# Decode block with cached attention: three equal rooms of 64 KB rows for the load stream, one batch per partition half, last heads' work regrouped

## The chip, the cores and the metric

One core of one Trainium2 chip. The metric is the device time of one execution in microseconds, as the median of several runs; the kernel before has 698.93 us (three runs, 698.74 to 699.79). All times in the profile are counted from the start of one profiled execution.

## What is computed

One decode step of a transformer block with adaptive layer norm, for two batches (B = 2) of one token of width 512, all in float32. Attention has 32 heads of width 128 over a cache of 4096 positions; the hidden layer has 1376 units. Cut to what matters:

```python
mod = (silu(c) @ w_mod).reshape(2, 6, 1, 512)          # sa, ca, ga, sb, cb, gb
h = layernorm(x) * (1 + ca) + sa
q = (h @ wq) per head
p = softmax(q . k_cache / sqrt(128))                    # 4096 positions
x = x + ga * ((p . v_cache) over all heads @ wo)
h = layernorm(x) * (1 + cb) + sb
a = h @ w1 + b1
x = x + gb * ((a * tanh(softplus(a))) @ w2)
```

The two caches are 268 MB of the 297 MB that are read; every byte is used once. So a load stream runs through the whole kernel, and the engines work beside it.

## The kernel before

**The stream.** `stream()` (lines 28 to 64) writes down the order of all loads by hand. The pieces are K of a head and V of a head (8192 float32 a partition each, `BIG`), a quarter chunk of wq or wo (2048, `W`, for four heads) and the other weights. K of head h is followed by V of an earlier head; at heads 14 and 22 (`AHEAD`) V is left out, so that V falls two heads further behind, and three V heads are left for after the last K. `load(n)` (line 136) issues load n on the SP queue into a room of SBUF. `room(n)` (line 115) gives every third load the one room of 48 KB a partition (`one`), and the others one of two rooms of 64 KB (`two`); a `one` room holds a K or V head and, in some, wq and wo chunks, a `two` room two heads. `used(*keys)` (line 148) issues the next load as soon as all pieces of the room three loads back have been used in program order; on the chip SP then waits until the engines are done with that room. The program lists 53 input transfers.

**Batches.** Each partition holds 32 positions of batch 0 and 32 of batch 1 (`b j d`). The positions of a batch are spread over all 128 partitions.

**The loop over heads** (lines 432 to 454). For head h: `products` (L316) multiplies K by q in place on DVE, q being spread to all partitions by matmuls in `project_q` (L288, one set for each batch); `soft_max(h - 1)` (L337, L339) takes the maximum over partitions out of PSUM and makes the exponentials and their sums on ACT, once for each batch; `sums` (L319) reduces the products to scores; `row_max` (L324 to L331) takes the maxima, lays them on a diagonal (d, 128 x 256) and multiplies by ones, so that each partition sees all maxima. `weighted_v` (L365) makes p . V on PE: 16 calls for a head, each of 512 columns, four of them side by side in groups of 32 output rows; the trace shows each call as two matmuls. After four heads `value_sums` (L379) copies the sums out, `head_values` (L387) divides and turns them, and `project_o` (L395) multiplies by wo. The engines take their instructions in program order, so a matmul behind one that waits for a load waits too.

**The tail** (line 458 on). After the last K: the softmax of head 31; V of heads 29 and 30, then modulation 4 (L241, `modulation`: 16 calls), the output projection of heads 28 to 30 (`head_out_q`, L403), V of head 31, its sums, its projection; then xg = projection x mod 2 (L494), the second layer norm (`centred`, L194, with modulation 3 laid between), `h2t`, the w1 matmuls (L521), the activation (L548 to L556), the w2 matmuls (L561) and the output. `busy(n)` (L293) puts matmuls on PE whose result nobody reads. The last loads are: V28 with wo 6; V29; V30; wo 7 with m4; V31 in three parts; m3; w1 in two parts; m5; w2 in four parts (6, 3, 1 and 1 of its 11 chunks of 512). m0, m1 and m2 come first of all with wq 0 and 1.

Of the kernel before, what the change touches and what calls it, by code (L numbers as in the profile page):

```python
# [8 lines left out]
F32 = mybir.dt.float32  # L9
# [10 lines left out]
W = 2048  # L20
SIZES = {
    "k": BIG, "v": BIG, "wq": W, "wo": W, "m012": 3 * W, "m3": W, "m4": W, "m5": W,
    "w1": 4 * sum(WIDTHS), "w2": 512 * len(CHUNKS),
}
AHEAD = (14, 22)


def stream():

    behind, pieces = {}, [("k", 0)]
    for h in range(1, HEADS):
        pieces.append(("k", h))
        if h not in AHEAD:
            behind[h] = len(behind)
            pieces.append(("v", behind[h]))
    left = list(range(len(behind), HEADS))
    pieces += [("v", h) for h in left[:-1]]

    extra = {}
    for c in range(2, HEADS // HC):
        at = (pieces.index(("k", HC * c)) - 1) // 5 * 5
        extra[at] = [("wq", c), ("wo", c - 2)]
    extra[60] = [("wo", HEADS // HC - 2)]
    loads = [[([("m012", 0), ("wq", 0), ("wq", 1)], (3 * W, 2 * W))]]
    n = 0
    while n < len(pieces):
        m = 1 if n % 5 == 0 else 2
        keys = pieces[n : n + m]  # L50
        if keys[0] == ("v", left[0]) and m == 2:
            loads.append([([key], (BIG,)) for key in keys])
        else:
            keys = keys + (extra.pop(n, []) if m == 1 else [])
            loads.append([(keys, (sum(SIZES[kind] for kind, _ in keys),))])
        n += m
    assert not extra and len(loads) % 3 == 0
    last = HEADS - 1
    loads += [
        [([("wo", HEADS // HC - 1), ("m4", 0)], (2 * W,)), ([("v", last)], (BIG // 2, BIG // 4, BIG // 4))],  # L60
        [([("m3", 0), ("w1", 0)], (W, 2 * sum(WIDTHS), 2 * sum(WIDTHS)))],
        [([("m5", 0), ("w2", 0)], (W, 6 * 512, 3 * 512, 512, 512))],
    ]
    return loads, behind, left
# [3 lines left out]
def kernel(  # L68
# [5 lines left out]
    behind: dict,  # L74
    left: list,
# [19 lines left out]
    NS = BIG // (B * DH)  # L95
# [19 lines left out]
    def room(n):  # L115

        if n % 3 == 1:
            return kvp.tile([P, BIG + 2 * W], F32, tag="one", name=f"one{n}", bufs=1)
        return kvp.tile([P, 2 * BIG], F32, tag="two", name=f"two{n}", bufs=2)

    def take(t, keys):
        lo = 0
        for kind, n in keys:
            part = t[:, lo : lo + SIZES[kind]]
            lo += SIZES[kind]
            if kind in "kv":
                (k_t if kind == "k" else v_t)[n] = part.rearrange("p (b j d) -> p b j d", b=B, d=DH)
# [8 lines left out]
    def load(n):  # L136

        t = room(n)
# [126 lines left out]
    ps = modulation("0", 3, w_t["m012"])  # L265
# [16 lines left out]
    def project_q(ch):  # L282

        q_t[ch] = work.tile([P, B, HC, DH], F32, tag="q", name=f"q{ch}")
        for b in range(B):
            ps = wide_ps(f"qps{ch}_{b}")
            for k in range(G):
                nc.tensor.matmul(  # L288
                    ps, lhsT=hc[:, k, b : b + 1].to_broadcast([P, P]), rhs=wq_t[ch][:, k, :], start=(k == 0), stop=(k == G - 1)
                )  # L290
            nc.scalar.activation(q_t[ch][:, b].rearrange("p h d -> p (h d)"), ps, AF.Copy, scale=SCALE)  # L291

    def busy(n):  # L293

        for lo in range(0, n, 2):
            cols = P * min(2, n - lo)
            nc.tensor.matmul(ov[1][:, :cols], lhsT=ident, rhs=e_t[0][0].rearrange("p c m -> p (c m)")[:, :cols], start=True, stop=True)
# [5 lines left out]
    s_t, m_t, mps, l_t, lps, pick_t, o_t = {}, {}, {}, {}, {}, {}, {}  # L303

    e_t = [[const.tile([P, NB, R], F32, name=f"e{i}_{b}") for b in range(B)] for i in range(HC)]
    ot_t = [const.tile([P, HC, R], F32, name=f"ot{i}") for i in range(2)]
    for t in sum(e_t, ot_t):
        nc.gpsimd.memset(t, 0.0)
# [12 lines left out]
    def row_max(h):  # L321

        m_t[h] = work.tile([P, 4], F32, tag="m", name=f"m{h}")
        nc.vector.tensor_reduce(out=m_t[h][:, 0:2], in_=s_t[h], axis=AX.X, op=ALU.max)  # L324
        d = work.tile([P, B, P], F32, tag="d", name=f"d{h}", bufs=1)
        nc.vector.tensor_tensor(  # L326
            out=d, in0=ident[:, None, :].to_broadcast([P, B, P]),
            in1=m_t[h][:, 0:2, None].to_broadcast([P, B, P]), op=ALU.mult,
        )
# [311 lines left out]
```

## Time and profile before

| | |
|---|---|
| median of the runs | 698.93 us |
| span of the profiled execution | 697.0 us |
| around it (launch and end), median less span | 1.9 us |
| DVE busy | 595.8 us (85%) |
| PE busy | 308.2 us (44%) |
| ACT busy | 43.7 us (6%) |
| input read | 297.2 MB, 426 GB/s over the span |
| mean granted clock of TensorE | 0.713 |

The profiled execution has no time of its own beside its span; the 1.9 us are taken from the median. A row of the profile names the line, the engine, the operation, the tile written and the tiles read, and its shape; then comes the busy time, the mean of one, and the idle time of that engine ahead of it with what ended it. PEld is TensorE's weight load, which overlaps its matmuls. In a row of the timeline the first number is the start and the second the duration. "DMA share" is the mean busy share of the 16 DMA engines. "PEclk" is the clock granted to TensorE, 1 being full.

### The profile page before, as it was taken

The page shows a single profiled execution, that of the slowest core. Times are in us where ns is not written, and L with a number is a line of the kernel's source. Part 1 is how long each engine was busy: PE and PEld are TensorE (multiplying, and loading weights), DVE is VectorE, ACT ScalarE, POOL GpSimd, SP SyncE. Part 2 cuts the span into 40 slices and gives each one's busy share as a digit, 9 for nine tenths or more (in the row PEclk, how much of TensorE's full clock was granted, in tenths as well). Part 3 has the DMA queues.
Part 4 walks back from the last instruction along what each step waited for, and adds up shares of the span by engine and source line. Part 5 has one row for each costly group of instructions (what it writes and reads, how often), then busy time and mean ns, then how long its engine had stood idle before and what let it go on. Part 6 is the DMA issues. An engine that isn't in the chain of part 4 may idle for free.

```text
span 697.0 us, 4072 instructions
## 1 busy us (share of the span) xinstructions
PE 308.2 (44%) x1692; PEld 107.0 (15%) x1692; DVE 595.8 (85%) x218; ACT 43.7 (6%) x176; POOL 4.4 (1%) x22
## 2 busy tenths in 40 slices
PE   2913343523453722843034831644043832226686
PEld 1300011100110200310011200211010300002234
DVE  3399999959999769999999789999999689999501
ACT  1100000000000000010000100000000100000001
POOL 2000000000000000000000000000000000000000
PEclk9966656776556765695665865986556975666799
DMA  9999999999999999999999999999999999999996
GB/s 383 453 429 417 427 459 411 448 429 416 454 432 425 438 425 428 448 430 433 429 444 426 432 440 417 446 432 429 444 423 440 430 425 440 429 420 432 422 422 269
DMA packets 7842, 297.48 MB, mean 427 GB/s; under 512 B 1016, under 2 KB 1040, under 8 KB 1424
## 3 DMA queue, kind: packets, MB, share of 16 engines
q1 hardware_dynamic: 7648, 297.21, 98.9%
q8 instruction: 13, 0.21, 0.1%
q10 hardware_dynamic: 176, 0.01, 0.0%
q14 instruction: 5, 0.04, 0.0%
HBM read 297.22 MB, written 0.00 MB: 426 GB/s over the span
## 4 chain that ended last, share of the span: by engine, by line
DVE 72%; DMA 24%; PE 2%; issue 1%; POOL 0%; SPq 0%; ACT 0%; DVEq 0%; POOLq 0%
DVE s L319 35%; DVE two L316 25%; DMA two<-in_load 22%; DVE one L316 10%; DMA bias<-in_b1c 2%; DVE d L326 1%; PE qps L288 1%; PE modps L241 1%; DVE m L324 1%; DVE m L337 0%; DVE pick L357 0%; SPq L143 0%; DVE pick L356 0%; PE fps L263 0%; ACT q L291 0%
## 5 line engine op out<-in xcount | busy, mean ns | idle before, releaser
L316 DVE TENSOR_TENSOR two<-two,q 128x8192 f32<-128x8192 f32 x24 | 208.5, 8687 | 37.1 <-DMA two<-in_load 37.1
L319 DVE TENSOR_REDUCE s<-two 128x64 f32<-128x8192 f32 x24 | 208.2, 8675 | 0.0
L365 PE MATMUL ov<-two,e 128*32 128x512 f32 x864 | 148.0, 847 | 134.1 <-DMA two<-in_load 81.9
L331 PE MATMUL mt<-d,ones 128*128 128x256 f32 x64 | 28.6, 536 | 130.3 <-DVE d L326 130.3
L316 DVE TENSOR_TENSOR one<-one,q 128x8192 f32<-128x8192 f32 x8 | 69.5, 8685 | 7.9 <-ACT q L291 7.9
L365 PEld LDWEIGHTS ov<-two,e 128*32 128x32 f32 x864 | 33.8, 149 | 233.4 <-issue 110.3
L319 DVE TENSOR_REDUCE s<-one 128x64 f32<-128x8192 f32 x8 | 69.4, 8676 | 0.0
L339 ACT ACTIVATE e<-s,m 128x32 f32<-128x32 f32 x64 | 20.1, 314 | 483.0 <-DVE m L337 483.0
L288 PE MATMUL qps<-one,hc 128*128 128x512 f32 x96 | 45.0, 624 | 0.0
L365 PE MATMUL ov<-one,e 128*32 128x512 f32 x160 | 28.1, 867 | 32.8 <-ACT e L339 17.1
L331 PEld LDWEIGHTS mt<-d,ones 128*128 128x128 f32 x64 | 12.0, 235 | 153.5 <-DVE d L326 108.9
L348 PE MATMUL l<-l,ones 128*128 128x8 f32 (+2 forms) x18 | 5.4, 370 | 63.4 <-ACT e L339 63.4
L288 PEld LDWEIGHTS qps<-one,hc 128*128 128x128 f32 x96 | 18.9, 201 | 24.4 <-issue 24.1
L348 PEld LDWEIGHTS l<-l,ones 128*128 128x128 f32 x18 | 4.5, 312 | 68.9 <-ACT e L339 68.5
L337 DVE TENSOR_REDUCE m<-mt 128x2 f32<-128x256 f32 x32 | 13.4, 418 | 1.4 <-PE mt L331 1.4
L326 DVE TENSOR_TENSOR d<-ident,m 128x256 f32<-128x256 f32 x32 | 13.6, 425 | 1.1
L365 PEld LDWEIGHTS ov<-one,e 128*32 128x32 f32 x160 | 6.3, 154 | 52.0 <-ACT e L339 17.9
L288 PE MATMUL qps<-two,hc 128*128 128x512 f32 x32 | 14.0, 595 | 0.3 <-DVE hc L278 0.3
L387 PE MATMUL otp<-pick,o 128*128 128x8 f32 (+2 forms) x72 | 10.0, 264 | 7.6 <-DVE m L324 4.7
L291 ACT ACTIVATE q<-qps 128x512 f32<-128x512 f32 x16 | 9.4, 594 | 52.2 <-PE qps L288 52.2
L339 ACT ACTIVATION_READ_ACCUMULATOR e<-s,m 128x1 f32 x64 | 12.0, 187 | 0.0
L387 PEld LDWEIGHTS otp<-pick,o 128*128 128x128 f32 x72 | 9.2, 200 | 14.8 <-ACT o L379 9.1
(105 smaller groups left out, 95.0 us busy)
## 6 DMA issues: line engine op xcount, KB each, us to landing
one<-in_load SPq DMA_DIRECT2D x6, 6144.0 KB, 31.8
one<-in_load SPq DMA_DIRECT2D x6, 4096.0 KB, 29.7
two<-in_load SPq DMA_DIRECT2D x2, 4096.0 KB, 24.7
two<-in_load SPq DMA_DIRECT2D x3, 2048.0 KB, 14.8
one<-in_load SPq DMA_DIRECT2D x1, 5120.0 KB
two<-in_load SPq DMA_DIRECT2D x1, 3072.0 KB
two<-in_load SPq DMA_DIRECT2D x3, 1024.0 KB, 20.7
one<-in_load SPq DMA_DIRECT2D x2, 1376.0 KB
```

The costliest lines, as they stand in the source:

```text
L241: nc.tensor.matmul(ps[R * g : R * (g + 1)], lhsT=ct[:, k, :], rhs=t[:, k, :].rearrange("p (m n) -> p m n", m=n)[:, :, P * g : P * (g + 1)] ...
L288: nc.tensor.matmul(ps, lhsT=hc[:, k, b : b + 1].to_broadcast([P, P]), rhs=wq_t[ch][:, k, :], start=(k == 0), stop=(k == G - 1))
L291: nc.scalar.activation(q_t[ch][:, b].rearrange("p h d -> p (h d)"), ps, AF.Copy, scale=SCALE)
L316: nc.vector.tensor_tensor(out=k_t[h], in0=k_t[h], in1=qv, op=ALU.mult)
L319: nc.vector.tensor_reduce(out=s_t[h], in_=k_t[h], axis=AX.X, op=ALU.add)
L326: nc.vector.tensor_tensor(out=d, in0=ident[:, None, :].to_broadcast([P, B, P]), in1=m_t[h][:, 0:2, None].to_broadcast([P, B, P]), op=ALU.mult,
L331: nc.tensor.matmul(mps[h], lhsT=ones, rhs=d, start=True, stop=True)
L337: nc.vector.tensor_reduce(out=m[:, 2:4], in_=mps[h], axis=AX.X, op=ALU.max, negate=True)
L339: nc.scalar.activation(e_t[i][b][:, :, M * i + 4 * b : M * i + 4 * b + 4], s_t[h][:, b].rearrange("p (c m) -> p c m", m=4), AF.Exp, bias=m ...
L348: nc.tensor.matmul(lps[n][:, x], lhsT=ones, rhs=l_t[n][:, x], start=True, stop=True)
L365: nc.tensor.matmul(ov[bank][R * g : R * (g + 1), :], lhsT=e_t[h % HC][b][:, c, :], rhs=v_t[h][:, b, 4 * c : 4 * c + 4, :].rearrange("p m d ...
L387: nc.tensor.matmul(tps[:, x], lhsT=o_t[m], rhs=pick_t[n][:, m, x], start=(m == 0), stop=(m == 3),)
```

## The change

**One row for each load.** The rooms are three of 64 KB (`room`, line 132 after), and loads 1 to 31 are each one transfer of 64 KB a partition: one K head with as much of the following pieces as fits, where V now comes in halves of 4096 (the key is `("v", head, part)`) and a wq chunk goes with the wo chunk of two chunks earlier. Load 0 is m0 and m1 with wq 0 and 1 (32 KB), then K of head 0 (32 KB). The program lists 43 input transfers. The last ones are: V28 with wo 6; V29; V30; V31 whole; wo 7 with m2, m4 and m3; w1 whole; m5 with 5 chunks of w2; 4 chunks; 1; 1. To make room, the scratch for dynamic DMAs is set to 1024 bytes.

**One batch per partition half.** Partitions 0 to 63 hold batch 0, 64 to 127 batch 1, each with 64 positions. q is then one set of matmuls (`hcw` holds the 64 columns of each batch), the exponentials are made on 64 partitions for each batch with 64 positions each, and the maximum needs a d of 64 columns, multiplied by `same` (ones within a half). `e_t` is one tile for a head, `sum_t` two fixed tiles for the sums.

**The tail.** Modulation 0 at the start has two parts (m0, m1) rather than three; modulation 2 is now made in the tail. The sums of heads 28 to 31 are divided in one step. Order on PE: V29, V30, the sums of heads 28 to 30, V31, modulation 2, the projection of heads 28 to 30, the sums of head 31, half of modulation 4, the projection of head 31, the other half; within the layer norm m4 + 1 on DVE; modulation 3 whole after the variance, and `busy(2)` where six stood. The `busy` calls around head 31's sums are gone.

```diff
@@ -18,50 +18,48 @@
 HC = 4
 BIG = 8192
 W = 2048
+HALF = BIG // 2
 SIZES = {
-    "k": BIG, "v": BIG, "wq": W, "wo": W, "m012": 3 * W, "m3": W, "m4": W, "m5": W,
+    "k": BIG, "v": HALF, "wq": W, "wo": W, "m01": 2 * W, "m2": W, "m3": W, "m4": W, "m5": W,
     "w1": 4 * sum(WIDTHS), "w2": 512 * len(CHUNKS),
 }
 AHEAD = (14, 22)
+ROW = 2 * BIG
 
 
 def stream():
 
 
-
...
+    order, n_v = [], 0
     for h in range(1, HEADS):
-        pieces.append(("k", h))
+        order.append(("k", h))
+        if h % HC == HC - 1 and HC < h < HEADS - 1:
+            c = (h + 1) // HC
+            order.append([("wq", c), ("wo", c - 2)])
         if h not in AHEAD:
...
+            order += [("v", n_v, 0), ("v", n_v, 1)]
+            n_v += 1
+    order = [x if isinstance(x, list) else [x] for x in order]
+
+    def size(x):
+        return sum(SIZES[key[0]] for key in x)
+
+    loads = [[([("m01", 0), ("wq", 0), ("wq", 1)], (4 * W,)), ([("k", 0)], (BIG,))]]
+    for _ in range(1, HEADS):
+        row = []
+        while size(row) < ROW:
+            room = ROW - size(row)
+            row += order.pop(next(i for i, x in enumerate(order) if size(x) <= room))
+        loads.append([(row, (ROW,))])
+    last = [("v", h, i) for h in range(HEADS - 4, HEADS) for i in range(2)]
+    assert order == [[key] for key in last[:2]], order
     loads += [
...
+        [(last[:2] + [("wo", 6)], (BIG + W,))],
+        [(last[2:4], (BIG,)), (last[4:6], (BIG,))],
+        [(last[6:], (BIG,)), ([("wo", 7), ("m2", 0), ("m4", 0), ("m3", 0)], (4 * W,))],
+        [([("w1", 0)], (SIZES["w1"],)), ([("m5", 0), ("w2", 0)], (W + 5 * 512, 4 * 512, 512, 512))],
     ]
+    return loads
 
 
 @with_exitstack
@@ -135,7 +129,7 @@
 
     def load(n):
 
-        t = room(n)
+        t = kvp.tile([P, ROW], F32, tag="room", name=f"room{n}", bufs=3)
         lo = 0
         for keys, srcs in loads[n]:
             take(t[:, lo:], keys)
@@ -178,8 +172,17 @@
         out=mean_w, in0=fold[:, None, :].to_broadcast([P, G, R]), scalar1=1.0 / D, scalar2=None, op0=ALU.mult
     )
     mean_w = mean_w.rearrange("p g r -> p (g r)")
+    half = const.tile([P, PB], F32, name="half")
+    nc.vector.tensor_reduce(
+        out=half, in_=ident.rearrange("p (b r) -> p r b", b=B), axis=AX.X, op=ALU.add
+    )
+    same = const.tile([P, B, PB], F32, name="same")
     ones = const.tile([P, P], F32, name="ones")
     nc.vector.memset(ones, 1.0)
+    nc.vector.memset(same, 0.0)
+    for b in range(B):
+        nc.vector.memset(same[PB * b : PB * (b + 1), b, :], 1.0)
+    same = same.rearrange("p b r -> p (b r)")
     eps_t = const.tile([P, 1], F32, name="eps_t")
     nc.vector.memset(eps_t, EPS)
 
@@ -272,47 +275,46 @@
         mod[m] = const.tile([P, P], F32, name=f"mod{m}")
         nc.scalar.copy(mod[m], ps)
 
-    keep(2, ps[:, 2, :])
     hps = columns(hq, "hps")
-    hc = const.tile([P, G, B], F32, name="hc")
-    nc.vector.tensor_copy(hc, hps)
+    hcw = const.tile([P, G, B * PB], F32, name="hcw")
+    nc.vector.tensor_copy(
+        hcw.rearrange("p g (b r) -> p g b r", b=B), hps[:, :, :, None].to_broadcast([P, G, B, PB])
+    )
 
     q_t = {}
 
     def project_q(ch):
 
-        q_t[ch] = work.tile([P, B, HC, DH], F32, tag="q", name=f"q{ch}")
-        for b in range(B):
-            ps = wide_ps(f"qps{ch}_{b}")
-            for k in range(G):
-                nc.tensor.matmul(
-                    ps, lhsT=hc[:, k, b : b + 1].to_broadcast([P, P]), rhs=wq_t[ch][:, k, :], start=(k == 0), stop=(k == G - 1)
-                )
-            nc.scalar.activation(q_t[ch][:, b].rearrange("p h d -> p (h d)"), ps, AF.Copy, scale=SCALE)
+        q_t[ch] = work.tile([P, HC, DH], F32, tag="q", name=f"q{ch}")
+        ps = wide_ps(f"qps{ch}")
+        for k in range(G):
+            nc.tensor.matmul(ps, lhsT=hcw[:, k, :], rhs=wq_t[ch][:, k, :], start=(k == 0), stop=(k == G - 1))
+        nc.scalar.activation(q_t[ch].rearrange("p h d -> p (h d)"), ps, AF.Copy, scale=SCALE)
...
     def products(h):
 
-        s_t[h] = work.tile([P, B, NS], F32, tag="s", name=f"s{h}")
-        qv = q_t[h // HC][:, :, h % HC, None, :].to_broadcast([P, B, NS, DH])
+        s_t[h] = work.tile([P, NS], F32, tag="s", name=f"s{h}")
+        qv = q_t[h // HC][:, h % HC, None, :].to_broadcast([P, NS, DH])
         nc.vector.tensor_tensor(out=k_t[h], in0=k_t[h], in1=qv, op=ALU.mult)
@@ -320,55 +322,48 @@
 
     def row_max(h):
 
-        m_t[h] = work.tile([P, 4], F32, tag="m", name=f"m{h}")
-        nc.vector.tensor_reduce(out=m_t[h][:, 0:2], in_=s_t[h], axis=AX.X, op=ALU.max)
-        d = work.tile([P, B, P], F32, tag="d", name=f"d{h}", bufs=1)
-        nc.vector.tensor_tensor(
-            out=d, in0=ident[:, None, :].to_broadcast([P, B, P]),
-            in1=m_t[h][:, 0:2, None].to_broadcast([P, B, P]), op=ALU.mult,
-        )
-        mps[h] = small_ps(f"mt{h}")[:, : B * P].rearrange("p (b n) -> p b n", b=B)
-        nc.tensor.matmul(mps[h], lhsT=ones, rhs=d, start=True, stop=True)
+        m_t[h] = work.tile([P, 2], F32, tag="m", name=f"m{h}")
+        nc.vector.tensor_reduce(out=m_t[h][:, 0:1], in_=s_t[h], axis=AX.X, op=ALU.max)
+        d = work.tile([P, PB], F32, tag="d", name=f"d{h}", bufs=1)
+        nc.vector.tensor_scalar(out=d, in0=half, scalar1=m_t[h][:, 0:1], scalar2=None, op0=ALU.mult)
+        mps[h] = small_ps(f"mt{h}")[:, :PB]
+        nc.tensor.matmul(mps[h], lhsT=same, rhs=d, start=True, stop=True)
 
     def soft_max(h):
         m, n, i = m_t[h], h // HC, h % HC
-        if i == 0:
-            l_t[n] = work.tile([P, HC * B], F32, tag="l", name=f"l{n}", bufs=3)
-        nc.vector.tensor_reduce(out=m[:, 2:4], in_=mps[h], axis=AX.X, op=ALU.max, negate=True)
+        nc.vector.tensor_reduce(out=m[:, 1:2], in_=mps[h], axis=AX.X, op=ALU.max, negate=True)
         for b in range(B):
+            own_b = slice(PB * b, PB * (b + 1))
             nc.scalar.activation(
-                e_t[i][b][:, :, M * i + 4 * b : M * i + 4 * b + 4],
-                s_t[h][:, b].rearrange("p (c m) -> p c m", m=4),
-                AF.Exp, bias=m[:, 2 + b : 3 + b], accum_out=l_t[n][:, B * i + b : B * i + b + 1],
+                e_t[i][own_b, :, M * i + 4 * b : M * i + 4 * b + 4],
+                s_t[h][own_b].rearrange("p (c m) -> p c m", m=4),
+                AF.Exp, bias=m[own_b, 1:2], accum_out=sum_t[n % 2][own_b, B * i + b : B * i + b + 1],
             )
 
...
-    def weighted_v(h, b, bank, first=True, last=True):
-
-        for c in range(NB):
+    def weighted_v(h, part, bank, first=True, last=True):
+
+        for c in range(NB // 2):
             g = c % G
             nc.tensor.matmul(
                 ov[bank][R * g : R * (g + 1), :],
-                lhsT=e_t[h % HC][b][:, c, :],
-                rhs=v_t[h][:, b, 4 * c : 4 * c + 4, :].rearrange("p m d -> p (m d)"),
-                start=(first and b == 0 and c < G),
-                stop=(last and b == B - 1 and c >= NB - G),
+                lhsT=e_t[h % HC][:, NB // 2 * part + c, :],
+                rhs=v_t[h, part][:, c, :],
+                start=(first and part == 0 and c < G),
+                stop=(last and part == 1 and c >= NB // 2 - G),
             )
+        used(("v", h, part))
@@ -408,19 +403,17 @@
             )
 
 
-    along = {}
-    for parts in loads[1::3]:
-        for keys, _ in parts:
-            along[keys[0]] = keys[1:]
     ready, waiting = set(), []
 
-    def weights(key):
-        for kind, n in along.get(key, ()):
-            if kind == "wq":
-                project_q(n)
-                used((kind, n))
-            else:
-                waiting.append(n)
+    def values(h, part):
+        n, i = h // HC, h % HC
+        weighted_v(h, part, n % 2, i == 0, i == HC - 1)
+        if part == 1 and i == HC - 1:
+            value_sums(n % 2, (nc.scalar.copy,))
+            head_values(n)
+            ready.add(n)
+
+    def outputs():
         for n in [n for n in waiting if n in ready]:
             waiting.remove(n)
             project_o(n)
@@ -428,29 +421,30 @@
 
     project_q(0)
     project_q(1)
-    used(("m012", 0), ("wq", 0), ("wq", 1))
+    used(("m01", 0), ("wq", 0), ("wq", 1))
     for h in range(H):
+        with_k = [key for keys, _ in loads[h] for key in keys] if h else []
+        if h == H - 1:
+            with_k += loads[H][0][0]
         products(h)
         if h:
             soft_max(h - 1)
             if h % HC == 0:
                 totals(h // HC - 1)
-        weights(("k", h))
+        for key in with_k:
+            if key[0] == "wq":
+                project_q(key[1])
+                used(key)
+            elif key[0] == "wo":
+                waiting.append(key[1])
         sums(h)
         if h and h % HC == 0:
             denominators(h // HC - 1)
         used(("k", h))
-        if h in behind:
-            v = behind[h]
-            n, i = v // HC, v % HC
-            for b in range(B):
-                weighted_v(v, b, n % 2, i == 0, i == HC - 1)
-            used(("v", v))
-            if i == HC - 1:
-                value_sums(n % 2, (nc.scalar.copy,))
-                head_values(n)
-                ready.add(n)
-            weights(("v", v))
+        for key in with_k:
+            if key[0] == "v":
+                values(*key[1:])
+            outputs()
         row_max(h)
 
 
@@ -465,26 +459,22 @@
             start=True, stop=False, skip_group_check=True,
         )
     soft_max(H - 1)
-    for part in ((0, HC - 1), (HC - 1, HC)):
-        totals(N, *part)
-        denominators(N, *part)
-    for h in left[:-1]:
-        for b in range(B):
-            weighted_v(h, b, N % 2, False, h == H - 2)
-        used(("v", h))
+    totals(N)
+    denominators(N)
+    for h in range(H - 3, H - 1):
+        for part in range(2):
+            weighted_v(h, part, N % 2, False, h == H - 2)
     value_sums(N % 2, (nc.scalar.copy,))
-    mps4 = modulation("4", 1, w_t["m4"])
-    m4 = work.tile([P, P], F32, tag="xn", name="m4", bufs=1)
-    nc.vector.tensor_scalar(out=m4, in0=mps4[:, 0, :], scalar1=1.0, scalar2=None, op0=ALU.add)
     head_values(N, 0, HC - 1)
+    for part in range(2):
+        weighted_v(H - 1, part, 1 - N % 2)
+    value_sums(1 - N % 2, (nc.scalar.copy, nc.vector.tensor_copy))
+    ps = modulation("2", 1, w_t["m2"])
+    keep(2, ps[:, 0, :])
     for h in range(HC * N, H - 1):
         head_out_q(h)
-    for b in range(B):
-        weighted_v(H - 1, b, 1 - N % 2)
-    value_sums(1 - N % 2, (nc.scalar.copy, nc.vector.tensor_copy))
-    busy(2)
     head_values(N, HC - 1, HC)
-    busy(1)
+    mps4 = modulation("4", 1, w_t["m4"], ks=(0, 1))
     head_out_q(H - 1)
     wm3, wm5 = w_t["m3"], w_t["m5"]
     w1_t, w2_t = w_t["w1"], w_t["w2"]
@@ -496,14 +486,15 @@
     def add_x(total):
         nc.vector.scalar_tensor_tensor(x2, xg, 1.0, xq, op0=ALU.mult, op1=ALU.add, accum_out=total)
 
-    mps3 = modulation("3", 1, wm3, ks=(0, 1))
+    m4 = work.tile([P, P], F32, tag="xn", name="m4", bufs=1)
 
     def more_work():
-        modulation("3", 1, wm3, mps3, (2, 3))
-        busy(1)
-
+        nc.vector.tensor_scalar(out=m4, in0=mps4[:, 0, :], scalar1=1.0, scalar2=None, op0=ALU.add)
+
+    modulation("4", 1, w_t["m4"], mps4, (2, 3))
     xc, var, rs = centred(x2, "b", add_x, more_work)
-    busy(6)
+    mps3 = modulation("3", 1, wm3)
+    busy(2)
     nc.vector.tensor_tensor(out=m4, in0=xc, in1=m4, op=ALU.mult)
     y0, y1 = rstd(var, rs)
     nc.scalar.activation(xc, m4, AF.Copy, scale=y0)
```

More of the change, by code (lines that the diff above doesn't have):

```diff
@@ L296, in busy @@
             cols = P * min(2, n - lo)
-            nc.tensor.matmul(ov[1][:, :cols], lhsT=ident, rhs=e_t[0][0].rearrange("p c m -> p (c m)")[:, :cols], start=True, stop=True)
+            nc.tensor.matmul(ov[1][:, :cols], lhsT=ident, rhs=e_t[0].rearrange("p c m -> p (c m)")[:, :cols], start=True, stop=True)
     NB = NS // 4
@@ L601, in _lay_out, with piece @@
         w2[: f1 - f0, n] = a["B_w2"][f0:f1]
-    pieces = {**kv, "wq": wq, "wo": wo, "m012": [wm[:, :, :1536]], "w1": [w1], "w2": [w2]}
-    for n in (3, 4, 5):
+    pieces = {**kv, "wq": wq, "wo": wo, "m01": [wm[:, :, :1024]], "w1": [w1], "w2": [w2]}
+    for n in (2, 3, 4, 5):
         pieces[f"m{n}"] = [wm[:, :, 512 * n : 512 * (n + 1)]]
+    def piece(kind, n, part=None):
+        row = pieces[kind][n].reshape(P, -1)
+        return row if part is None else row[:, HALF * part : HALF * (part + 1)]
     arrays = {
@@ L609, in _lay_out @@
     }
-    for n, parts in enumerate(stream()[0]):
+    for n, parts in enumerate(stream()):
         for i, (keys, widths) in enumerate(parts):
-            row = np.concatenate([pieces[kind][m].reshape(P, -1) for kind, m in keys], axis=1)
+            row = np.concatenate([piece(*key) for key in keys], axis=1)
             cuts = np.split(row, np.cumsum(widths)[:-1], axis=1)
@@ L630 @@
         ).ap()
-    loads, args["behind"], args["left"] = stream()
+    loads = stream()
     args["loads"] = [
```

76 lines of the change are left out of this document (22 added, 54 removed).

## The prediction

> **What bounds the kernel now.** I read four views in this order: the page's head and its DMA queues, a table of stages, the end of the chain of waits, and the timeline of the last 50 us. A time or duration below is in us from the start of the profiled execution; sizes are elements of a partition (float32, 128 partitions, so 512 elements are 0.262 MB).
>
> The page's head, and the row of the load queue (packets, MB, share of the 16 DMA engines' time):
>
> ```profile
> span 697.0 us, 4072 instructions
> q1 hardware_dynamic: 7648, 297.21, 98.9%
> ```
>
> Two stages: busy times of PE, PEld, DVE, ACT, POOL, then the granted clock, the DMA share and GB/s.
>
> ```profile
> 3.00:660.00 657.00, 279.67 (x1324) 91.32 (x1328) 589.55 (x195) 40.51 (x164) 1.54 (x7) 0.70 1.00 432
> 660.00:693.00 33.00, 28.14 (x368) 15.51 (x360) 4.29 (x20) 3.23 (x12) 0.42 (x1) 0.95 0.95 394
> ```
>
> The load stream fills the DMA engines (share 1.00 at 432 GB/s over 657 us). DVE, busy 589.55 of those 657, is the next engine, and it waits for data. So a gain in the loop cannot come from any engine's work; only from fewer bytes (they stay at 297.2 MB), a cheaper stream, or the two ends. The end of the chain of waits (start, us, what):
>
> ```profile
> 653.77 20.74 DMA two<-in_load
> 674.53 18.52 DMA two<-in_load
> 693.09 0.47 PE yps L561 x8
> 693.66 0.30 DVE y L569
> ```
>
> Here the kernel waits for its last load until 693.09, and 3.9 us follow that no edit touches. The median of the runs, 698.93, is 1.9 us above this execution's span; I add that to each span. Within 0.2% (1.4 us) a time counts as the same.
>
> **The change, part by part: the stream.** Before issues 53 input transfers, after 43, of the same bytes. What one boundary costs is bounded from the tail, where five short transfers follow each other:
>
> ```profile
> 683.66 0.97 PEld L521 LDWEIGHTS w1ps<-one,h2t 128*32 128x32 f32 x16 [0.32 <-DMA one<-in_load]
> 690.04 1.52 PE L561 MATMUL yps<-two,actt 128*32 128x128 f32 x48 [0.81 <-DMA two<-in_load]
> 691.80 1.08 PE L561 MATMUL yps<-two,actt 128*32 128x128 f32 x32 [0.25 <-DMA two<-in_load]
> 693.09 0.42 PE L561 MATMUL yps<-two,actt 128*32 128x128 f32 x8 [0.21 <-DMA two<-in_load]
> ```
>
> The first row starts when the second half of w1 is there, the last when the last load is. Between them 2048 + 3072 + 1536 + 512 + 512 elements arrive: 3.93 MB in 9.43 us, where 432 GB/s would take 9.10. That is 0.07 us a transfer. The low end is 0 (the queue is full, the share 1.00). The high end lays all that the second stage falls short on its transfers: 33.0 us at 394 GB/s are 13.0 MB, 30.1 us at 432, so 2.9 us over about 12, 0.24 each. I take 0.07, the directly measured one: ten fewer boundaries save 0.7 us (0 to 2.4). The last load is then there at 692.4.
>
> **Does the stream stay full with three equal rooms?** A row of 16384 elements (8.39 MB) takes 19.4 us at 432 GB/s, and each row from 1 to 31 brings one K head. DVE's work for a head:
>
> ```profile
> L316 DVE TENSOR_TENSOR two<-two,q 128x8192 f32<-128x8192 f32 x24 | 208.5, 8687 | 37.1 <-DMA two<-in_load 37.1
> L319 DVE TENSOR_REDUCE s<-two 128x64 f32<-128x8192 f32 x24 | 208.2, 8675 | 0.0
> L337 DVE TENSOR_REDUCE m<-mt 128x2 f32<-128x256 f32 x32 | 13.4, 418 | 1.4 <-PE mt L331 1.4
> L326 DVE TENSOR_TENSOR d<-ident,m 128x256 f32<-128x256 f32 x32 | 13.6, 425 | 1.1
> 47.47 0.22 DVE L324 TENSOR_REDUCE m<-s 128x2 f32<-128x64 f32 x1
> 47.46 0.33 SPq L143 DMA_DIRECT2D one<-in_load  x1
> bias<-in_b1c ACTq DMA_DIRECT2D x1, 6.0 KB, 12.1
> ```
>
> 8.69 + 8.68 + 0.42 + 0.43 + 0.22 is 18.4, with some overlap 18.3 from head to head. The batches by halves leave the two long ones as they are; d and the maximum over mt shrink from 256 to 64 columns, so a head costs between 17.4 (the long two alone) and 18.3. I take 17.9. DVE therefore keeps ahead of the 19.4 us rows by 1.1 to 2.0 us, and gains nothing for the end by it. A room is free when its head's sums are done, at most 18.3 after its row landed if DVE has no backlog; the V matmuls of the row are done sooner (32 of them take 6.2 us, row 640.34 below). The two other rooms hold 38.8 us of stream, so the next load is queued about 20 us before it is needed. At the start the backlog is largest. Before frees the room of head 0 at 47.46 (SP row). Row 0 now lands near 21, with a smaller modulation (two thirds) and half the matmuls for q ahead of head 0; against that the small load of b1, which took 12.1 us beside the first rows (last row above) and stands ahead of the modulation on PE, may come later beside longer rows. Even at 47.5 that is 12 us before row 2 has landed (1.8 + 3 x 19.4 = 60). So I cost the rooms, the halved q projection, the shorter softmax pieces and the constants at nothing: the full stream hides them, with 12 us of cover at the start and 20 later.
>
> **The tail.** Counting back from 692.4 with 432 GB/s and 0.07 a transfer: after the transfer of wo 7, m2, m4 and m3 come 5504 + 4608 + 2048 + 512 + 512 elements, 6.75 MB, 15.6 + 0.35 us, so it lands at 676.4; V31 at 666.6, w1 at 682.9, m5 with the first part of w2 at 688.5. Before had wo 7 and m4 ahead of V31 and m2 at the start, so that only V31's last quarter and m3 were left for here. After 676.4 PE now has in order: modulation m2 (16 calls, which the trace shows as 32 matmuls), the output projection of heads 28 to 30 (24), the sums of head 31 (8), half of m4 (16), and the projection of head 31 (8). Only then can xg start. Rows of before for each:
>
> ```profile
> 664.66 1.08 PE L241 MATMUL modps<-two,ct 128*32 128x128 f32 x32
> 666.99 0.86 PE L403 MATMUL xps<-two,ot 128*32 128x128 f32 x24 [0.26 <-ACT ot L390]
> 676.17 1.07 PE L387 MATMUL otp<-pick,o 128*128 128x2 f32 x8
> 677.27 0.16 ACT L390 COPY ot<-otp 128x2 f32<-128x2 f32 x1 [1.15 <-PE otp L387]
> 677.49 0.43 PE L403 MATMUL xps<-two,ot 128*32 128x128 f32 x8
> 677.98 0.29 DVE L494 TENSOR_TENSOR xg<-xps,mod 128x128 f32<-128x128 f32 x1 [1.41 <-PE xps L403]
> ```
>
> At full clock, with about 0.2 us of each row being pipeline tail: 676.4 + 0.87 + 0.65 + 1.07 + 0.25 (copy and start) + 0.43 + 0.06 gives xg at 679.7. That is 1.7 later than 677.98. mod 2's copy (0.27 on ACT) lies beside the projections; m4 + 1 moves into DVE's wait for the variance (0.29 of a wait of 0.6).
>
> But PE will not be at full clock. V31, 32 matmuls, starts at 666.6 after an idle stretch and ends by 673; PE then has nothing until 676.4. What such a stretch does is in these rows (two windows of 3.41 us cut at the steps of the granted clock, which is the third number from the end; then the same 8 matmuls as 677.49 at half clock, V matmuls partly at half clock, and two starts of a group of four):
>
> ```profile
> 666.07:669.48 3.41, 1.52 (x30) 1.17 (x30) 0.04 (x1) 0.17 (x1) 0.00 (x0) 1.00 0.97 406
> 669.48:672.89 3.41, 3.31 (x16) 0.79 (x20) 0.00 (x0) 0.00 (x0) 0.00 (x0) 0.50 1.02 423
> 654.36 0.66 PE L463 MATMUL xps<-att_sb,fold 128*32 128x128 f32 x8
> 640.34 6.22 PE L365 MATMUL ov<-one,e 128*32 128x512 f32 x32 [4.38 <-DMA one<-in_load]
> 657.99 0.19 PEld L365 LDWEIGHTS ov<-two,e 128*32 128x32 f32 x4 [0.66 <-issue]
> 661.62 0.12 PEld L365 LDWEIGHTS ov<-two,e 128*32 128x32 f32 x4 [0.31 <-issue]
> ```
>
> A window with PE busy 1.52 of 3.41 us put the next at clock 0.50; a busy one brought 1.00 back. At 0.50 a group starts every 0.85 us, not 0.43. The idle stretch 673 to 676.4 holds such a window, so I expect the tail to begin at 0.50 and to stay there until a busy window has ended: 3.4 to 6.8 us after 676.4 by where the window's edge falls, somewhat less if a mostly busy window is enough. The walk above, 3.3 us at full clock, costs half of that stay more: 1.3 (2.7 us at half clock) to 3.0 (nearly all of it); I take the middle, 2.2. xg is then at 681.0 to 682.7, likeliest 681.9: 3.9 late. [...]
>
> From xg to the end the steps are those of before: 4.57 to the w1 matmuls, then 2.77, the copies, fps, mod 5 and the filler.
>
> ```profile
> 682.55 2.77 PE L521 MATMUL w1ps<-one,h2t 128*32 128x384 f32 x32
> 687.66 1.56 PE L297 MATMUL ov<-e,ident 128*128 128x256 f32 x6
> 688.16 0.20 DVE L556 TENSOR_TENSOR actt<-f 128x22 f32<-128x22 f32 x1
> ```
>
> The whole m3 (1.08) and two filler columns now stand where six fillers stood (1.54), an even exchange. What was slack in before: actt was ready at 688.4 and PE at 689.2, but the last matmuls waited for w2 until 690.04 (0.8), and were spread over the landings until 693.5, where together they take about 2.6 instead of 3.5 (0.9). So 1.7 of the 3.9 us are absorbed. **Sum:** the end comes 2.2 us later by this walk, less about 0.2 of rounding in overlaps where I doubt the pipeline tails: +2.0, span 699.0, time 700.9. At the two ends of the clock's delay: 700.0 and 701.9.
>
> **The rivals.** *The tail stays hidden.* If PE keeps its clock, xg is 1.7 late, the slack is 1.7, and the load bounds the end: between -0.7 (the stream's saving alone, 698.2) and +0.4 (699.3). For it: the slack nearly equals the delay. Against it: 666.07 to 669.48, where a shorter idle stretch cost the clock.
>
> *The boundaries are dearer than they look (faster).* Each boundary might leave engines idle for p us. Time is 700.9 - (10p - 0.7), as a shorter stream moves the landing at 676.4 too; faster by 1.4 us needs p of 0.41, so 697.5 or less. The rows allow 0.24 at most, which gives 699.2. With the share at 1.00 I hold that for unlikely. [...]
>
> *The loop loses the stream (slower).* DVE becomes the bound if a head costs over 19.4 us, 1.1 more than now, or if rooms come free late. At 19.8 a head DVE ends about 663, the room for V31's row is free then and not at 656.8 when the stream needs it, and the time is about 707. Against it: the two long rows are unchanged and the small ones shrink.
>
> **How the numbers follow.** The late tail 0.67, of which 0.07 lie within 0.2%; hidden tail 0.20; dearer boundaries 0.05; lost stream 0.08. So faster 0.05, same 0.27, slower 0.68. The range goes from the hidden tail's low end, 698.2, to the late tail with nothing saved in the stream, 701.9 + 0.7 = 702.6; the lost stream and the dear boundaries are left out. The late tail's own range is 700.0 to 701.9.
>
> **What would show it.** Of the changed profile: DMA share 1.00 at 432 GB/s from 3 to 655; heads 19.4 us apart with DVE waiting before each product; the m2 modulation starting near 676.4 at clock 0.50; xg near 682; the w1 matmuls and the last matmuls waiting for PE and DVE and no longer for a load; the last matmuls in one piece of about 2.6 us. A gap in the DMA share between rows, a wait for a load at the last matmuls, or a granted clock of 1.00 at 676 would prove me wrong.

## The result, and the profile after

The changed kernel takes 704.34 us (median of four runs), the kernel before 699.12 in the same series: a ratio of 1.0078, with a 95% interval of 1.0063 to 1.0092. The prediction had the direction and the place; 700.9 was forecast, up to 702.6, so 3.4 us of the 5.2 lost were not in it.

The page's head and load queue of the changed kernel, then the same two stages as before (PE, PEld, DVE, ACT, POOL busy; granted clock, DMA share, GB/s):

```profile
span 702.5 us, 3939 instructions
q1 hardware_dynamic: 6208, 297.21, 98.1%
```

```profile
3.00:660.00 657.00, 259.15 (x1278) 87.37 (x1282) 581.17 (x197) 40.59 (x155) 1.42 (x4) 0.66 1.00 432
660.00:693.00 33.00, 25.72 (x242) 14.63 (x234) 3.16 (x14) 2.61 (x9) 0.42 (x1) 0.65 0.92 388
```

The first stage is the one of before to the digit: share 1.00, 432 GB/s. What differs is the granted clock of the second, 0.65 after 0.95. The end of the chain of waits shows where the time is (start, us, what):

```profile
643.85 33.07 DMA room<-in_load
676.96 1.94 PE modps L244 x32
678.90 1.28 PE xps L398 x24
680.18 1.80 PE otp L382 x8
681.98 1.01 PE modps L244 x16
682.99 0.43 PE xps L398 x8
683.41 0.90 PE modps L244 x16
...
689.97 2.76 PE w1ps L512 x16
...
696.58 2.58 PE yps L552 x88
```

Before, this chain was DMA up to 693.09 and then one group of matmuls. Now DMA ends at 676.96, with wo 7, m2, m4 and m3, and the rest is PE with a few steps of DVE between. Nothing after 676.96 waits for a load. Five rows of the timeline of that stretch (start, us, what, idle time ahead and what ended it):

```profile
683.55 0.29 DVE L484 TENSOR_TENSOR xg<-xps,mod 128x128 f32<-128x128 f32 x1 [9.06 <-PE xps L398]
686.19 1.93 PE L244 MATMUL modps<-room,ct 128*32 128x128 f32 x32
688.25 0.35 DVE L501 SCALAR_TENSOR_TENSOR hq<-xc_b,rs_b,modps 128x128 f32<-128x128 f32 x1 [0.98 <-PE modps L244]
689.90 2.77 PE L512 MATMUL w1ps<-room,h2t 128*32 128x384 f32 x32
696.50 2.61 PE L552 MATMUL yps<-room,actt 128*32 128x128 f32 x88
```

And the windows of 3.41 us cut at the steps of the clock, which is again the third number from the end:

```profile
672.62:676.03 3.41, 0.91 (x8) 0.00 (x0) 0.42 (x1) 0.37 (x1) 0.00 (x0) 1.00 0.97 415
676.03:679.45 3.42, 2.49 (x48) 2.31 (x52) 0.00 (x0) 0.27 (x1) 0.00 (x0) 0.50 0.96 412
679.45:682.86 3.41, 3.41 (x44) 2.92 (x40) 0.00 (x0) 0.16 (x1) 0.42 (x1) 0.50 1.04 436
682.86:686.27 3.41, 2.54 (x36) 1.96 (x32) 1.68 (x8) 0.00 (x0) 0.00 (x0) 0.50 0.97 413
686.27:689.68 3.41, 3.41 (x37) 2.74 (x38) 0.95 (x5) 0.86 (x3) 0.00 (x0) 0.50 0.89 365
689.68:693.10 3.42, 3.00 (x34) 1.65 (x33) 0.10 (x1) 0.29 (x2) 0.00 (x0) 1.00 0.29 109
```

The clock falls at 676.03, at the end of a window with PE busy 0.91 us, and comes back only at 689.68, four windows later. The third row is the surprise: PE is busy for all of its 3.41 us, and the next window still has 0.50.

Two rows from the loop, and two from its start, for the steps that were costed at nothing:

```profile
158.16 0.25 DVE L328 TENSOR_SCALAR d<-half,m 128x64 f32<-128x64 f32 x1
159.75 8.69 DVE L318 TENSOR_TENSOR room<-room,q 128x8192 f32<-128x8192 f32 x1 [1.34 <-DMA room<-in_load]
```

```profile
49.84 0.33 SPq L137 DMA_DIRECT2D room<-in_load  x1
bias<-in_b1c ACTq DMA_DIRECT2D x1, 6.0 KB, 17.5
```

DVE waits 1.34 us for a row once it has caught up; the room of head 0 is free at 49.84, 10 us before the 60 at which the prediction has row 2 landed, although the load of b1 took 17.5 us rather than 12.1.

### The profile page after: what moved, and what is told of

Its sections match the earlier page's. It is cut to its first block, busy times and chain, and to the rows that moved or that the text cites. A ratio compares the mean times of both kernels' runs of the same rounds, so it can differ in the third digit from the quotient of the medians.

```text
span 702.5 us, 3939 instructions
## 1 busy us (share of the span) xinstructions
PE 290.7 (41%) x1648; PEld 107.0 (15%) x1648; DVE 587.4 (84%) x220; ACT 44.1 (6%) x168; POOL 4.2 (1%) x20
## 4 chain that ended last, share of the span: by engine, by line
DMA 59%; DVE 35%; PE 4%; issue 0%; POOL 0%; ACT 0%; ACTq 0%; SPq 0%; DVEq 0%; POOLq 0%
DMA room<-in_load 56%; DVE s L321 17%; DVE room L318 17%; DMA bias<-in_b1c 2%; PE modps L244 1%; PE qps L291 1%; PE ov L298 0%; PE w1ps L512 0%; PE yps L552 0%; PE otp L382 0%; PE xps L398 0%; DVE m L334 0%; DVE m L326 0%; PE fps L527 0%; DVE d L328 0%
## 5 line engine op out<-in xcount | busy, mean ns | idle before, releaser
L318 DVE TENSOR_TENSOR room<-room,q 128x8192 f32<-128x8192 f32 x32 | 278.1, 8691 | 40.3 <-DMA room<-in_load 34.2
L321 DVE TENSOR_REDUCE s<-room 128x64 f32<-128x8192 f32 x32 | 277.9, 8684 | 0.0
L359 PE MATMUL ov<-room,e 128*32 128x512 f32 x1024 | 177.4, 851 | 72.0 <-ACT e L337 27.8
L330 PE MATMUL mt<-d,same 128*128 128x64 f32 x64 | 18.8, 388 | 200.4 <-DVE d L328 200.4
L359 PEld LDWEIGHTS ov<-room,e 128*32 128x32 f32 x1024 | 39.3, 147 | 182.5 <-issue 131.5
L337 ACT ACTIVATE e<-s,m 64x64 f32<-64x64 f32 x64 | 22.1, 345 | 551.1 <-DVE m L334 550.3
L330 PEld LDWEIGHTS mt<-d,same 128*128 128x128 f32 x64 | 13.5, 263 | 230.3 <-DVE d L328 183.9
L291 PE MATMUL qps<-room,hcw 128*128 128x512 f32 x64 | 43.9, 852 | 4.8 <-DMA room<-in_load 4.0
L291 PEld LDWEIGHTS qps<-room,hcw 128*128 128x128 f32 x64 | 17.0, 276 | 26.9 <-issue 20.9
L337 ACT ACTIVATION_READ_ACCUMULATOR e<-s,m 64x1 f32 x64 | 11.8, 185 | 0.0
```

What stands on the lines that cost most here:

```text
L291: nc.tensor.matmul(ps, lhsT=hcw[:, k, :], rhs=wq_t[ch][:, k, :], start=(k == 0), stop=(k == G - 1))
L318: nc.vector.tensor_tensor(out=k_t[h], in0=k_t[h], in1=qv, op=ALU.mult)
L321: nc.vector.tensor_reduce(out=s_t[h], in_=k_t[h], axis=AX.X, op=ALU.add)
L330: nc.tensor.matmul(mps[h], lhsT=same, rhs=d, start=True, stop=True)
L337: nc.scalar.activation(e_t[i][own_b, :, M * i + 4 * b : M * i + 4 * b + 4], s_t[h][own_b].rearrange("p (c m) -> p c m", m=4), AF.Exp, bias ...
L359: nc.tensor.matmul(ov[bank][R * g : R * (g + 1), :], lhsT=e_t[h % HC][:, NB // 2 * part + c, :], rhs=v_t[h, part][:, c, :], start=(first a ...
```

## The experiments

Three theories stood at the start. **Clock:** the tail's work behind the last weights runs at half clock, because PE idles ahead of it. **Amount:** there is too much PE work behind that landing, whatever the clock. **Loop:** the rooms or the halves cost the stream time. Each ratio is to the kernel before, run beside it. In the code cuts `...` stands for lines left out.

**Gap filled (e1).** Seven calls of the idle product between V31 and modulation 2:

```diff
+    busy(14)
     ps = modulation("2", 1, w_t["m2"])
```

> The changed kernel with seven idle-product matmul calls (busy(14)) on PE between V31 and modulation 2, where PE waited from 673.5 to 677.0. Clock theory (the tail's PE chain runs at half clock because PE idles before the m2 landing): granted clock 1.00 at 677, xg at 680.3 rather than 683.6, w1 matmuls at 685, time 699 to 700. Amount theory (too much PE work lies behind that landing, whatever the clock): xg stays near 683, time 703.5 to 704.5. Loop theory (the stream lost time to rooms or halves): no change, 704.3.

Measured: 700.85 us, ratio 1.0019 (1.0007 to 1.0031). Two clock windows, then xg and the last matmuls of the profiled run:

```profile
672.86:676.27 3.41, 3.41 (x21) 2.42 (x14) 0.42 (x1) 0.37 (x1) 0.00 (x0) 1.00 0.89 380
676.27:679.69 3.42, 3.36 (x75) 2.75 (x77) 0.00 (x0) 0.32 (x2) 0.41 (x1) 1.00 1.03 442
```

```profile
680.53 0.29 DVE L485 TENSOR_TENSOR xg<-xps,mod 128x128 f32<-128x128 f32 x1 [5.96 <-PE xps L398]
691.70 2.61 PE L553 MATMUL yps<-room,actt 128*32 128x128 f32 x88
```

The clock stays 1.00, xg comes 3.0 us sooner and the last matmuls 4.8 us sooner, with the same loads and the same useful work. The profiled run took 699.51; the ten runs lie between 699.35 and 702.67, and what lengthened the others no trace shows. The median is a little above the 699 to 700 that the clock theory gave, far from the 704 of the others. Fillers alone give back 3.5 of the 5.2 us, by the medians.

**m2 early (e2).** m2 is loaded beside V28 and its modulation made before V29:

```diff
-        [(last[:2] + [("wo", 6)], (BIG + W,))],
+        [(last[:2] + [("wo", 6), ("m2", 0)], (BIG + 2 * W,))],
-        ... ([("wo", 7), ("m2", 0), ("m4", 0), ("m3", 0)], (4 * W,))],
+        ... ([("wo", 7), ("m4", 0), ("m3", 0)], (3 * W,))],
...
```

> The changed kernel with m2 loaded beside V28 and wo 6 and its modulation made before V29, so that 32 matmuls leave the tail; the number of bytes and the landing of the last pieces stay. Clock theory: the clock is still 0.50 behind the landing, which now lies 2.4 us later in the walk's favour only by the 1.94 us of the m2 matmuls: time 702 to 703. Amount theory: the same 2 us, or the whole 5 if m2 alone was what made the tail late. Loop theory: no change, 704.3.

Measured: 701.47 us, ratio 1.0032 (1.0023 to 1.0041), 0.5 below the range. The clock did not do what I wrote:

```profile
675.39:678.80 3.41, 2.40 (x40) 1.43 (x32) 0.42 (x1) 0.37 (x1) 0.07 (x1) 1.00 1.03 441
678.80:682.22 3.42, 2.20 (x51) 1.88 (x54) 1.67 (x8) 0.16 (x1) 0.34 (x1) 1.00 1.00 427
682.22:685.63 3.41, 3.41 (x38) 2.84 (x38) 1.00 (x6) 0.87 (x3) 0.00 (x0) 0.50 0.98 418
```

With 2048 elements less behind V31, V31 itself arrives later (its matmuls start at 669.80, not 667.24) and the gap to the next weights is 1.0 us, not 3.4. So the clock is kept over the landing and lost later, at 682.22; this is the profiled run, 700.24, and the ten reach 702.50. The run cannot part amount from clock, since it changes both.

**Tail of before (e3).** Rooms, rows and halves of the changed kernel; order on PE, fillers and last loads of the kernel before, with m2 loaded beside V28:

```diff
+        [([("wo", 7), ("m4", 0)], (2 * W,)), (last[6:], (BIG // 2, BIG // 4, BIG // 4))],
+        [([("m3", 0), ("w1", 0)], (W, 2 * sum(WIDTHS), 2 * sum(WIDTHS))), ([("m5", 0), ("w2", 0)], (W, 6 * 512, 3 * 512, 512, 512))],
...
```

> The changed kernel (three equal rooms, rows of 64 KB, one batch per partition half) with the tail of before: order on PE, fillers, and wo 7 and m4 ahead of a V31 in three parts; m2 beside V28. Clock and amount theories: all of the loss is in the tail, so 698.3 to 699.2. Loop theory: the rooms and halves cost the time, so 703 to 704.5.

Measured: 699.09 us, ratio 0.9993 (0.998 to 1.0005). The last matmuls wait for the last load again, at the time of before (693.09):

```profile
690.03 1.52 PE L556 MATMUL yps<-room,actt 128*32 128x128 f32 x48 [0.78 <-DMA room<-in_load]
693.11 0.43 PE L556 MATMUL yps<-room,actt 128*32 128x128 f32 x8 [0.22 <-DMA room<-in_load]
```

**New tail alone (e4).** The kernel before with the last loads and the PE order of the changed one:

```diff
-        [([("wo", HEADS // HC - 1), ("m4", 0)], (2 * W,)), ([("v", last)], (BIG // 2, BIG // 4, BIG // 4))],
+        [([("v", last)], (BIG,)), ([("wo", HEADS // HC - 1), ("m2", 0), ("m4", 0), ("m3", 0)], (4 * W,))],
...
```

> The kernel before with nothing but the new tail: load order and order on PE of the changed kernel behind the last K, m2 moved there. Clock and amount theories: 703.5 to 705. Loop theory: 698.5 to 699.5.

Measured: 704.84 us, ratio 1.0084 (1.0069 to 1.0099). Its windows are those of the changed kernel:

```profile
676.04:679.46 3.42, 2.40 (x48) 2.23 (x52) 0.00 (x0) 0.27 (x1) 0.00 (x0) 0.50 0.99 425
679.46:682.87 3.41, 3.41 (x41) 2.94 (x37) 0.00 (x0) 0.16 (x1) 0.42 (x1) 0.50 1.00 426
```

Together e3 and e4 close the loop theory: the whole loss goes with the tail and comes with it; three rooms, 64 KB rows and halves make no difference that is measured.

**Narrow fillers (e5).** What does a window need to count as busy? As e1 and with the same `ident` as the weights, but each of 16 calls streams 2 columns:

```diff
+    for _ in range(16):
+        nc.tensor.matmul(ov[1][:, :2], lhsT=ident, rhs=e_t[0].rearrange("p c m -> p (c m)")[:, :2], start=True, stop=True)
```

> The changed kernel with fillers between V31 and modulation 2 as in the gap-fill run, but each of 16 calls has 2 moving columns rather than 256. PE then shows as busy through the gap just the same. If what keeps the clock is that PE has instructions under way, the clock is 1.00 at 677 and the time is that of the gap-fill run, 699.5 to 701. If what counts is columns streamed, the clock falls to 0.50 at about 676 as in the changed kernel, and the time is 704 to 705.

Measured: 705.76 us, ratio 1.0087 (1.0062 to 1.0112).

```profile
672.74:676.15 3.41, 3.41 (x32) 2.61 (x24) 0.42 (x1) 0.37 (x1) 0.00 (x0) 1.00 0.89 380
676.15:679.56 3.41, 3.41 (x39) 3.28 (x42) 0.00 (x0) 0.00 (x0) 0.00 (x0) 0.50 0.99 418
```

The first row shows PE busy for the whole window, as in e1, and yet the next window is at 0.50. So it is not time under way that the clock follows: of that window 2.61 us were matmuls of 2 columns, and they did not hold it. The time itself says less, since the fillers run on to 678.2 and modulation 2 starts 1.15 us later than in the changed kernel (678.11); the profiled run, 706.72, is the longest of four, the shortest being 703.74.

**Head 31's sums early (e6).** Its 8 matmuls of 2 columns move ahead of modulation 2, with no filler:

```diff
+    head_values(N, HC - 1, HC)
     ps = modulation("2", 1, w_t["m2"])
     keep(2, ps[:, 0, :])
     for h in range(HC * N, H - 1):
         head_out_q(h)
-    head_values(N, HC - 1, HC)
```

> The changed kernel with the 8 two-column matmuls of head 31's sums moved ahead of modulation 2, into the time in which PE waits; no filler. Streamed-columns theory: the first window after the landing that is wholly busy now holds only wide matmuls and brings the clock back, near 683 rather than 689.7; xg at 681, time 699.5 to 701. Amount theory (only the 1.9 us of those matmuls leave the walk): clock 0.50 until 686 or later, time 702 to 703.

Measured: 700.17 us, ratio 1.0014 (1.0004 to 1.0023), in the range of the streamed-columns theory.

```profile
675.91:679.32 3.41, 2.56 (x49) 2.37 (x53) 0.00 (x0) 0.27 (x1) 0.00 (x0) 0.50 0.98 420
679.32:682.73 3.41, 3.34 (x56) 2.67 (x46) 0.59 (x3) 0.00 (x0) 0.00 (x0) 0.50 1.00 420
682.73:686.14 3.41, 2.61 (x40) 1.93 (x40) 2.13 (x10) 0.87 (x3) 0.00 (x0) 1.00 0.96 408
```

The second window is no busier than in the changed kernel (3.34 against 3.41 us), but only 0.56 us of it are narrow matmuls (two of 1 column), against 1.87 us of 2-column ones there; the rest has 128 columns, and the clock is back at 682.73, not 689.68. Moving eight matmuls saves 4.2 us by the medians. The profiled run, 3.7 us shorter, shows where: landing to xg takes 4.6 us rather than 6.6, since the eight are no longer in that walk; xg to the w1 matmuls takes 4.8 rather than 6.35, since the clock is back; the landing is 0.2 sooner.

**Fillers of before removed (e7).** In the kernel before:

```diff
-    busy(2)
     head_values(N, HC - 1, HC)
-    busy(1)
     head_out_q(H - 1)
...
-        busy(1)
...
-    busy(6)
```

> The kernel before without the idle-product matmuls of its tail up to the w1 matmuls (busy 2, 1, 1 and 6 go; V31 in three parts stays). If those fillers hold the clock there, it falls to 0.50 between 676 and 683 and the time is 700 to 702. If the small distance between V31's last part and the projections is enough, the clock stays 1.00 and the time is that of before, 699.3.

Measured: 699.93 us, ratio 1.0015 (1.0003 to 1.0026): between the two expectations, and just short of the lower bound of the first.

```profile
676.00:679.41 3.41, 2.46 (x43) 2.12 (x47) 1.15 (x5) 0.41 (x2) 0.42 (x1) 1.00 1.03 433
679.41:682.83 3.42, 1.86 (x21) 1.37 (x13) 1.54 (x8) 0.86 (x3) 0.00 (x0) 0.50 1.02 425
```

In the profiled run the clock does fall without them, at 679.41, and the w1 matmuls take 4.21 us. Most of that goes into the slack ahead of the last matmuls: this run took 699.27, level with before (699.19). Five of the ten runs lie at 699.3 to 699.4 like it, five at 700.4 to 702.0; what lengthened these, and so lifts the median by 0.7, no trace shows.

**Boundaries (e8).** The e3 kernel with each 64 KB row in two transfers:

```diff
-        loads.append([(row, (ROW,))])
+        loads.append([(row, (BIG, BIG))])
```

> The old-tail run (equal rooms, halves, tail of before; 699.1) with each of the 31 rows of 64 KB a partition loaded by two transfers of 32 KB: 31 boundaries more. At 0.07 us a boundary, as the prediction took: 701.3. At its upper bound of 0.24: 706.5. [...] At nothing: 699.1.

Measured: 701.82 us, ratio 1.0035 (1.0023 to 1.0047); 2.7 us over e3 for 31 boundaries, 0.09 us each (an estimate across two series; by the ratios it is 2.9 us, by the profiled spans, 700.1 and 697.1, it is 3.0).

**A short walk (e9).** The changed kernel's loads with m2 early, head 31's sums ahead of the landing and wide fillers (`busy(2)`, `busy(4)`) around them, and modulation 3 and fillers laid around the variance:

```diff
+    busy(2)
+    head_values(N, HC - 1, HC)
+    busy(4)
+    for h in range(HC * N, H):
+        head_out_q(h)
...
```

> The changed kernel with its 43 transfers and its last loads, but a short walk behind the last weights: m2 beside V28 and its modulation made early (as in the m2-early run), head 31's sums ahead of the landing (as in the sums-early run), fillers of 256 columns between V31 and the landing and within the layer norm. Clock theory: granted clock 1.00 from 676 on, xg at 678, the last matmuls wait for loads again, and the time is the load stream's: 698.3 to 699.0, level with before or 0.1% under it. If something else in the new tail costs time: 700 or more.

Measured: 701.04 us, ratio 1.0016 (1.0004 to 1.0027). A miss of 2 us: xg was at 678.6, but the end was lost elsewhere.

```profile
686.85:690.27 3.42, 2.01 (x39) 1.75 (x40) 1.14 (x6) 0.48 (x5) 0.00 (x0) 1.00 0.86 342
690.27:693.68 3.41, 3.41 (x22) 2.36 (x26) 0.00 (x0) 0.23 (x1) 0.00 (x0) 0.50 0.20 76
```

```profile
689.10 1.08 PE L244 MATMUL modps<-room,ct 128*32 128x128 f32 x32 [1.34 <-DMA room<-in_load]
690.11 2.81 PE L298 MATMUL ov<-e,ident 128*128 128x256 f32 x6
692.85 2.99 PE L557 MATMUL yps<-room,actt 128*32 128x128 f32 x88
```

PE, now early, waits 1.34 us for m5, which comes in one transfer with 5 chunks of w2; the clock is lost with that window (PE busy 2.01 of 3.41 us), and the six fillers behind it, meant to hold the clock, stand 2.81 us in front of the last matmuls.

**The filler moved (e10).** As e9, with the wait for m5 filled and nothing behind it:

```diff
+    busy(4)
     gps = modulation("5", 1, wm5)
...
-    busy(6)
```

> The short-walk run (701.0) with the fillers that stand between modulation 5 and the last matmuls (busy 6) gone and two such calls put ahead of modulation 5, where PE waits 1.3 us for m5. In the short-walk run the clock fell to 0.50 at 690.3 and the fillers took 2.81 us ahead of the last matmuls. Clock theory: clock 1.00 to the end, the last matmuls start near 690.2 and wait for loads, time 698.4 to 699.4, level with before. If the fillers themselves hold the clock for the last matmuls: 700 to 701.

Measured: 698.48 us, ratio 0.9986 (0.9977 to 0.9996).

```profile
689.13 1.08 PE L244 MATMUL modps<-room,ct 128*32 128x128 f32 x32 [0.18 <-DMA room<-in_load]
690.00 1.30 PE L557 MATMUL yps<-room,actt 128*32 128x128 f32 x40
691.52 1.75 PE L557 MATMUL yps<-room,actt 128*32 128x128 f32 x48 [0.21 <-DMA room<-in_load]
```

```profile
687.97:691.38 3.41, 3.15 (x77) 2.46 (x76) 1.13 (x6) 0.49 (x2) 0.00 (x0) 1.00 0.65 257
```

The window over the wait for m5 now has PE busy for 3.15 us rather than 2.01, and the clock stays 1.00 to the end. The last matmuls wait for loads again, the span is 696.7, and this version is 0.14% faster than the kernel before (0.04 to 0.23%) and 5.9 us faster than the change by the medians; its eleven runs lie within 0.3 us. That is what the change is worth once its tail is out of the way; the run does not part rooms, halves and the 43 transfers.

## Why the prediction was wrong

**Right.** The stream stays full and the loop gains nothing (share 1.00 at 432 GB/s; e3). The late tail is the mechanism, at its place: m2's modulation starts at 676.96 (676.4 forecast) at clock 0.50, no load is waited for after it, and the last matmuls run in one piece of 2.61 us (2.6). From the w1 matmuls to the end it takes 12.6 us where before took 14.5, so the slack that absorbs the delay is 1.9 us (1.7, with 0.2 for overlaps). Splitting a row costs 0.09 us a boundary (0.07 taken from the tail of before); e8 excludes the upper bound of 0.24.

**Wrong.** The step that failed is how long the clock stays down: "to stay there until a busy window has ended: 3.4 to 6.8 us after 676.4". It stayed for 13.65 us, 676.03 to 689.68, four windows. Term by term, against the forecast span of 699.0:

- the landing: 676.96, not 676.4, 0.6 us more. I had counted the load's arrival back from a last load at 692.4 with the whole saving of ten boundaries, 0.7 us. The traces show less of it: the stream's last bytes move at 692.2 here and at 692.5 in before, 0.3 us sooner, and e3, with 48 transfers, five fewer than before, waits for its last load until 693.11, before until 693.09. Why fewer boundaries gave back so little, when splitting rows costs 0.09 each, stays open
- from the landing to xg: 6.6 us, not 5.5 (3.3 and 2.2 for the clock), 1.1 more: all of the walk ran at 0.50, and about 0.3 of it is not the clock, since e1 takes 3.65 us for the same walk at 1.00 where the sum had 3.3
- from xg to the w1 matmuls: 6.35 us, not 4.57, 1.8 more. The prediction called the whole m3 against six fillers "an even exchange", which it is at full clock only: e1, at 1.00, takes 4.57 from xg to the w1 matmuls. At 0.50 m3 takes 1.93 us and hq waits 0.98 for it; the filler call behind it (`busy(2)`), 1.22, holds up h2ps.

Together 3.5 us, which makes 702.5, the measured span. One sum of the prediction is off by tenths, without bearing on this: xg at 682.7 is 4.7 late, which less the 1.9 us of slack and overlaps gives 701.7, not 701.9.

Why the clock stayed is shown for its main part. I took PE busy as what the clock follows. The window from 679.45 was busy from end to end and did not bring the clock back; 1.87 us of it are the eight matmuls of 2 columns. e6 takes just these out of that place, and the clock is back one window after; e5 puts such matmuls into the gap, PE is as busy as in e1, and the clock falls. The profile before already held such a window, in the loop:

```profile
286.82 1.52 PE L387 MATMUL otp<-pick,o 128*128 128x8 f32 x8 [1.78 <-DVE m L324]
287.19:290.60 3.41, 3.41 (x10) 2.49 (x11) 3.41 (x2) 0.17 (x1) 0.00 (x0) 0.50 0.89 384
290.60:294.02 3.42, 3.42 (x5) 1.35 (x4) 3.42 (x1) 0.00 (x0) 0.00 (x0) 0.50 1.20 517
```

PE was busy from end to end, 1.15 us of it in matmuls of 8 columns, and the next window still had 0.50. The prediction took its rule from one busy window, 669.48 to 672.89 (PE busy 3.31 us), which held matmuls of 512 columns alone; the next window had 1.00. The PE column of a profile does not tell such a window from the one at 287.19. Where exactly between 2 and 128 columns the weight lies was not tried. The window's edge moves between profiled runs: the clock steps at 676.03 in the changed kernel, at 682.22 in e2 and at 690.27 in e9, which are not whole windows of 3.41 us apart (6.19 and 8.05 us). Whether that is what spreads the runs of e1, e2 and e7 over 2.4 to 3.3 us is not shown, as each has one trace.

**The rivals.** The tail did not stay hidden, though e1 shows that it nearly would have with the clock kept (1.0019). The dearer boundaries and the lost stream are excluded by e8 and by e3.

## What to carry to other kernels

Where a chain of small matmuls stands behind the last loads, walk it at both clocks, and count as activity only what streams many columns (here 128 and more did, 2 did not): a PE column that reads busy from end to end can still sit at half clock (here 3.41 of 3.41 us, with 0.50 there and in the next window). Before moving a weight's load to the end, list the work that becomes its successor, and put everything that does not need it (here the sums of head 31) into the wait ahead of it; that one move gave back 4.2 of 5.2 us, about half of it as a shorter walk and most of the rest as clock. A filler belongs into a wait; behind it, in program order, it is work on the path, at nearly twice its length when the clock has already dropped (2.81 us in e9, 1.56 at full clock in before).

## What the runs showed that was not expected

- A window with PE busy 3.41 of 3.41 us, 1.87 us of it in 2-column matmuls, left the clock at 0.50; one with PE busy 3.34 us, 0.56 of it in 1-column and the rest in 128-column matmuls, brought it to 1.00.
- Sixteen calls of 2 columns (32 matmuls, 4.6 us) in a gap did not hold the clock; seven calls of 256 columns (14 matmuls, 3.3 us) did.
- Splitting 31 rows of 64 KB a partition into rows of 32 KB costs 2.7 us in 699; the last matmuls wait for their load until 695.99, without the split until 693.11.
